# A fused window-attention and gated-MLP kernel: new hand-written orders for all engines, with own and preceding scores merged from the fifth block on

## The chip, the cores and the metric

The kernel runs on one core of a Trainium2 chip. Five engines work side by side, each through its own list of instructions in a fixed order: TensorE (PE in the profile; its weight loads are PEld), VectorE (DVE), ScalarE (ACT), GpSimd (POOL, "Pool" here) and SyncE (SP), which does nothing here but issue transfers. Transfers are carried out by 16 DMA engines. An engine's next instruction waits until its semaphores are reached; whatever stands behind it in that engine's list waits with it. Time is device microseconds for one execution, start to end.

## What is computed

Attention over a sliding window of 128 keys and 4 "sink" keys, for 4 batches of 8 heads, 768 tokens, 64 values per head; its output, 3072 tokens of 512 values, goes through a two-layer network with the gate h * sigmoid(1.702 h) and 2048 hidden values.

```python
scores = scale * np.matmul(q, k.transpose(0, 1, 3, 2))
keep = is_sink | in_window            # first 4 keys, or 0 <= query - key < 128
scores = np.where(keep, scores, -1e9)
a = np.exp(scores - scores.max(-1, keepdims=True))
a = a / (a.sum(-1, keepdims=True) + 1e-9)
x = (a @ v), heads side by side: 3072 x 512
h = x @ w_in                          # 512 x 2048
out = (h / (1 + np.exp(-1.702 * h))) @ w_out
```

## The kernel before

**Blocks, positions and groups.** The 3072 tokens are 24 blocks of 128, six for each batch. They are worked on in the order ORD (L26): blocks 0, 6, 12, 18 (the first of each batch, which have no preceding block and no separate sink), then 1, 2, 3, 4, 5, 7, 8 and so on. A place in that order is called a position here, from 0: position 4 is block 1, 5 is block 2, 6 is block 3, 7 is block 4, 8 is block 5, 9 is block 7, 10 is block 8, 11 is block 9, 12 is block 10, 13 is block 11. Two positions make a group: group 2 is positions 4 and 5, group 4 is positions 8 and 9.

**One block's way.** Pool loads q, k and v, cast to 16 bits (L298, L289; block 0's q and k come through SyncE and ScalarE and are cast on the chip). q and k are transposed: on TensorE with an eviction by VectorE or ScalarE for positions 0 to 7 (L391), by a DMA transposition issued by SyncE for two positions at once from 8 on (L412). TensorE makes the scores against the block's own keys (`own`), against the preceding block's (`prv`) and against the four sink keys (L490). Only one of own and prv counts for each pair of query and offset, so VectorE picks between the two with a mask (`pack`, L514), takes the maximum (L526, L542), subtracts it (L583, L598), and ScalarE takes the exponential (L616; the first four positions take half of it from the scores directly, L569, and have their mask added on TensorE, L438). The result `a` is transposed into `at`: on TensorE for positions 0 to 3 (L679), by a DMA transposition issued by SyncE from position 4 on (L717). Pool then splits it into the weights for the preceding block and for the own block by two selects (L628, L622), 1.1 us each. TensorE multiplies with v (the "attention" of a position, in two halves `av0` and `av1`: L738 for the sinks, which uses `vsb`, then L744 and L748), VectorE normalises (L759, L760), and the result goes to `xT` by a TensorE transposition and an eviction (L773; positions 0 to 7) or a DMA transposition (L786; from group 4 on).

`vsb` is made once for each batch by VectorE or Pool (L346) from the first four rows of v, which SyncE loads (`vsa`, L341); every position from 4 on needs that of its batch.

**The network.** For each group TensorE does the first layer in eight parts `h0` to `h7` of 8 matmuls (group 0: 16 short ones each, four parts for each of its two blocks), ScalarE the gate on each (L838), and TensorE the second layer in two rows of four parts, `o0.0` to `o1.3` (L859), of which part n needs the gates of parts 2n and 2n + 1 and the quarter n of w_out. VectorE or ScalarE evicts, SyncE stores (L877). The exponential and the gate each need their own table on ScalarE; a change of table takes 1.28 us (ACT_TABLE_LOAD).

**What sets the order.** Every operation is added to a plan with a number (in the order in which the source adds them), a cost and a list of what it depends on. The plan's costs, margins (`late`, `post`), keys and `deps` were used to search for an order; in this file the result is written out, and nothing reads them any more. `ORDER` (L40) lists the operations by number with the engine's letter (P, A for ScalarE, V for VectorE, G for Pool, S for SyncE), and the last lines of the function emit them in that order; the tile framework then puts the semaphores, from the order of emission and from what each instruction reads and writes. Where two operations touch the same PSUM bank, the later one in the list waits for the earlier. `FILL` puts that many extra matmuls on zeros in front of an operation on TensorE, and `HOME` moves PSUM tiles from their usual ring of banks to another (`mm`, 3 banks, for transposes and the network; `own`, 2; `pv`, 2, for prv and av).

**Scores in one operation.** From position CFG["merge"] on, own and preceding scores are one operation (L466 to L478): its 16 matmuls alternate between the two, and it takes its four PSUM banks at once. Below, they are two operations.

**The order around the change, decoded.** TensorE, from the second-layer work of groups 0 and 1 on (S: scores, av: both halves where not numbered, Tx: transposition to xT): o1.3(g1) o1.2(g0) | av5 av4 | o1.3(g0) Tx5 av0-6 Tx4 S8 av1-6 | h of group 2, with sinks of 8 in between | Tx6 av7 o0.0 S9 o0.1 Tx7 ... Pool: loads q18, k18, the identity, q12, the mask bias0, k12, v18, v0, v6, q1, k1, v12, three parts of w_in, k2, q2, the fourth, q3, k3, k4, q4, four parts of w_out, q5, q7, k5, vsb of batch 1, v3, k7, v2, v1, then selects of positions 5, 4 and 6, six loads, select of 7, six loads, select of 8, two loads, select of 9. (k6 and q6 come first.) ScalarE: all 16 gates of groups 0 and 1, then the exponentials of positions 5, 4, 6, 7. SyncE: transpositions of `at` for 5 and 4, the load of vsa for batch 0, the transposition for 6, q and k of positions 8 and 9, and so on.

Of the kernel before, what the change touches and what calls it, by code (L numbers as in the profile page):

```python
# [29 lines left out]
PE, ACT, DVE, POOL, SP = "PE", "ACT", "DVE", "POOL", "SP"  # L30
CFG = dict(
    tq=(0, 1, 2, 3, 4, 5, 6, 7), ta=(0, 1, 2, 3), tx=tuple(range(8)), nb={0: 1, 1: 1, 2: 1, 3: 1}, wide=(1, 3),
    split=(0,), gbatch={}, tanh=(), after0=25.0, vsb=15.0, slack=dict(v=1.0, s=1.0, x=1.0, e=0.0, p=0.0), merge=8, pemask=(0, 1, 2, 3), f32=(0,), sel2=(), fill=(1.5, 45.0, 0.15, 0.11), chain=99, gap=3, steady=8, after=8.0,
# [7 lines left out]
9V 2V 18V 16V 4V 13V 19V 17V 12V 23G 0S 1S 7S 22G 28G 29G 3G 15V 11V 26G 21A 20V 108P 109V 110P 5G 10V 113P 27G 132P  # L41
133A 111V 112V 114P 130P 116V 32G 24G 25G 36G 37G 131A 118A 115V 31G 117V 174P 135P 136P 137V 119A 122P 175A 176P
139V 120P 138V 121V 152P 177A 154P 179P 33G 180P 123V 153A 141A 142P 155A 140A 35G 157P 182V 181V 184A 30G 41G 40G
124P 158P 183V 185A 159V 161V 126P 143A 34G 163A 144P 160V 127V 186P 162A 145V 187V 125V 164P 188P 146P 198P 189V
147V 165A 128P 129A 148P 149V 190P 191V 168P 196P 197A 192P 166P 150P 199A 582P 193V 194P 167V 169V 170P 151A 202P
590P 171V 583A 46G 47G 50G 49G 172P 173V 586P 594P 195A 178A 39G 38G 620P 591A 587A 595A 201P 200P 222P 612P 6S 203V
220P 221A 621A 614P 613A 615A 204V 223V 205V 206V 14V 207V 134V 208V 210V 608P 588P 592P 609A 589A 593A 209V 42G 43G
52G 55G 53G 584P 246P 618P 247V 585A 8S 101S 105G 48G 56G 45G 244P 270P 245V 225P 271V 224P 228V 610P 226P 619A 268P
580P 44G 616P 269A 581A 230V 227V 229V 231V 233V 622P 617A 232V 234V 248P 249P 251V 252V 253V 596P 623A 611A 235A
630P 250P 254V 255V 258V 256V 236S 631P 624P 257V 211A 259A 274P 597P 212S 625P 272P 273P 632P 275V 100S 260S 276V  # L50
277V 278V 279V 281V 626P 598P 280V 237G 627P 628V 292S 602P 599P 603P 213G 633P 282V 283A 604P 634A 635S 284S 600A
601S 104V 240P 261G 238P 241V 216P 214P 239V 605P 215V 217V 242P 62G 51G 606A 262P 243A 218P 607S 293P 219V 264P 58G
67G 65G 61G 285G 646P 294P 296V 295V 263V 297V 647A 265V 298V 299V 636P 640P 650P 300V 301V 302V 651A 648P 649A 644P
637A 645A 638P 642P 641A 639A 59G 266P 286P 288P 643A 267V 287V 289V 303A 652P 310P 312V 313V 653P 290P 57G 86G 54G
64G 68G 291A 304S 658P 314V 315V 311P 659P 328S 316V 674P 319V 318V 660P 317V 320A 676P 661P 664P 678P 677A 675A
321S 305G 71G 364S 662A 654P 73G 329P 665A 679A 102S 331V 322G 333V 655P 668P 669A 332V 308P 334V 672P 95G 309V 330P
325P 673A 74G 335V 306P 326V 666P 70G 323P 336V 337V 667A 670P 324V 307V 63G 79G 686P 671A 338V 327S 346P 339A 687P
680P 688P 347P 348V 349V 351V 350V 656A 340S 352V 353V 106G 681P 629S 355V 354V 689P 696P 356A 690A 382P 341G 60G
697A 657S 357S 384V 385V 682P 383P 692P 683P 386V 80G 693A 400S 103S 387V 388V 389V 390V 698P 694P 699A 78G 365P
695A 684A 702P 367V 358G 369V 704P 368V 370V 391V 705A 703A 700P 344P 366P 69G 76G 66G 77G 345V 371V 701A 361P 708P  # L60
392A 362V 359P 373V 714P 360V 342P 706P 393S 343V 372V 709P 715P 374V 363S 375A 418P 685S 707A 716P 376S 420V 394G
422V 710P 421V 436S 156A 717P 423V 419P 711P 718V 424V 425V 427V 722P 663S 712A 426V 83G 720P 726P 401P 723A 721A
728P 403V 724P 402P 729A 405V 377G 107V 75G 404V 725A 406V 730P 731A 72G 82G 88G 81G 397P 398V 407V 395P 732P 733A
727A 380P 734P 742P 396V 90G 408V 410V 428A 381V 378P 379V 736P 399S 743P 409V 411A 737P 735A 412S 454P 744P 456V
429S 738P 457V 713S 455P 739P 745P 458V 459V 89G 85G 472S 460V 413G 746A 462V 461V 748P 463V 437P 749A 754P 439V
752P 755A 430G 92G 414P 753A 740A 415V 440V 442V 441V 438P 758P 762P 750P 416P 443V 84G 96G 91G 94G 445V 433P 759A
756P 417V 444V 434V 751A 763A 770P 757A 464A 431P 764P 760P 432V 446V 435S 741S 490P 447A 765P 761A 448S 491P 766P
493V 492V 494V 495V 771P 465S 496V 499V 767P 768A 508S 691S 778P 769S 449G 497V 772P 779A 498V 788P 473P 789A 466G
784P 785A 475V 476V 474P 773P 477V 478V 479V 87G 98G 99G 452P 780P 781A 482V 774A 776P 467P 790P 97G 468V 481V 782P
791A 453V 777A 480V 469P 450P 786P 451V 470V 798P 787A 471S 775S 783A 526P 500A 792P 529V 528V 799P 527P 531V 530V  # L70
793P 483A 501S 532V 800P 533V 535V 794P 484S 534V 536A 806P 795P 807A 537S 502G 509P 801P 544S 511V 485G 802V 513V
796A 512V 510P 808P 505P 809A 810P 514V 747S 818P 811A 93G 506V 486P 538G 804P 487V 503P 805A 812P 816P 504V 813A
819A 515V 516V 517V 488P 814P 826P 489V 507S 815A 817A 562P 518V 519A 565V 564V 820P 827P 563P 520S 567V 566V 568V
828P 821P 571V 569V 829P 834P 570V 572A 545P 822P 830V 521G 835A 803S 831S 842P 573S 547V 548V 823P 843A 550V 549V
524P 824A 832P 546P 551V 554V 553V 846P 574G 525V 838P 847A 833A 552V 539P 540V 541P 840P 542V 844P 839A 841A 577P
836P 837A 848P 522P 523V 555A 854P 543S 849P 855P 845A 556S 850P 719S 797S 856P 575P 851P 557G 868P 576V 852A 857P
853S 869A 862P 858A 860P 870P 560P 861A 561V 863A 578V 866P 864P 871A 558P 865A 872P 559V 867A 882P 873A 876P 825S
579S 883P 877P 874P 878P 875A 884P 879P 892P 880V 885P 881S 893A 894P 886V 888P 887S 895A 859S 890P 889A 898P 891A
896P 899A 902P 910P 897A 900P 903A 911P 901A 904P 912P 905P 916P 906P 917P 907P 913P 908V 918P 914A 919P 909S 915S
920A 921S  # L80
# [3 lines left out]
    map(int, x.split(":"))  # L84
    for x in """
108:16 110:2 174:7 154:3 144:11 164:4 128:2
""".split()
)

HOME = dict(x.split(":") for x in "0:own 2:pv 6:own 8:own 10:pv 12:own 16:own 17:own 19:pv 20:pv 22:mm 25:own 26:own 27:mm 28:mm 29:own 32:pv 35:pv 38:own 39:pv 41:pv 43:own 45:own 46:mm 49:mm 50:mm 52:mm 53:mm 54:own 56:pv 57:mm 59:own 60:mm 61:mm 62:mm 64:own 66:mm 67:own 69:own 70:mm 168:own 170:pv 173:pv 174:own 177:pv 178:pv 179:pv 181:own 183:own 185:pv 187:pv 188:pv 191:pv 192:own 195:pv 197:pv 203:pv 204:own".split())  # L90

class Buf:


# [54 lines left out]
def kernel(  # L151
# [30 lines left out]
    plan = Plan(RING)  # L182
# [32 lines left out]
    raw, o_raw = {}, {}  # L215
# [709 lines left out]
```

## Time and profile before

| | us |
|---|---|
| median of 3 runs | 230.03 (230.0 to 230.13) |
| the profiled execution | 229.54 |
| its span in the profile | 227.8 |
| TensorE busy | 216.8 (95%) |
| VectorE, ScalarE, Pool busy | 136.0, 127.3, 114.3 |
| TensorE's granted clock | 1.00 in every stretch |
| the first matmul of the first layer | 20.79 |
| the end of the last matmul | 224.57 |

The profile shows one execution. Its page gives the engines' busy times, and the span in 40 slices of 5.7 us with the busy share of each in tenths. The timeline lists instructions with start and duration, merges equal neighbours (x8: eight of them), and says in brackets how long the engine had been idle before and what ended that: `[1.75 <-DVE vsb L346]` is 1.75 us idle until VectorE's instruction of line 346, which writes vsb, was done. `at<-a` reads: at is written from a. A row of SPq, the queue of SyncE, is the time that SyncE spent on issuing a transfer, not the transfer's own; "to landing" is from issue to the end of the transfer.

### The profile page before, as it was taken

How to read it: one execution, taken by the hardware profiler on the slowest of the kernel's cores; microseconds unless marked ns; L12 is line 12 of the kernel's file. 1: busy time of each engine (PE TensorE's matmuls, PEld its weight loads, DVE VectorE, ACT ScalarE, POOL GpSimd, SP SyncE). 2: the span in 40 equal slices, each digit the busy share in tenths (PEclk: the TensorE clock that was granted, in tenths of full speed). 3: DMA queues.
4: the chain of work that ended last, by engine and by line, in shares of the span. 5: the costliest groups of instructions: out<-in, count | busy, mean ns of one | idle time of the engine just before them, and what ended most of it. 6: DMA issues, size and time to landing. Idle time of an engine off the chain costs nothing.

```text
span 227.8 us, 5439 instructions
## 1 busy us (share of the span) xinstructions
PE 216.8 (95%) x2237; PEld 153.0 (67%) x2237; DVE 136.0 (60%) x334; ACT 127.3 (56%) x196; POOL 114.3 (50%) x126
## 2 busy tenths in 40 slices
PE   6789999996999999899999999999999999999994
PEld 4568998444785684585685695685695695775862
DVE  5799389674858188576875876577587751131101
ACT  2689675711584836757539359347646738441621
POOL 7995575118994594692794490570570430300000
PEclk9999999999999999999999999999999999999999
DMA  9999999999999999999999999998982703620302
GB/s 134 148 159 204 181 187 206 168 142 228 175 108 143 217 116 141 202 166 112 241 148 149 223 97 171 195 147 125 183 138 54 192 0 71 214 42 7 138 0 92
DMA packets 131992, 32.82 MB, mean 144 GB/s; under 512 B 124640, under 2 KB 129024, under 8 KB 131968
## 3 DMA queue, kind: packets, MB, share of 16 engines
q0 software_dynamic: 77024, 13.37, 77.6%
q1 hardware_dynamic: 53904, 18.85, 41.2%
q10 hardware_dynamic: 1040, 0.26, 0.5%
q8 instruction: 17, 0.28, 0.5%
q14 instruction: 7, 0.06, 0.1%
HBM read 27.36 MB, written 6.29 MB: 148 GB/s over the span
## 4 chain that ended last, share of the span: by engine, by line
PE 62%; DMA 16%; POOL 11%; issue 6%; DVE 1%; ACT 1%; POOLq 0%; SPq 0%
PE hT L808 28%; PE o L859 25%; DMA w_out<-in_moe_w_out_dram 6%; DMA w_in<-in_moe_w_in_dram 5%; POOL qkn L298 3%; DMA xT<-xn 3%; DMA at<-a 3%; POOL at L622 3%; POOL atp L628 2%; POOL v L289 2%; PE own L471 2%; PE av L744 2%; PE av L748 2%; PE av L738 1%; PE prv L471 1%
## 5 line engine op out<-in xcount | busy, mean ns | idle before, releaser
L808 PE MATMUL hT<-xT,w_in 128*128 128x256 f16 (+1 forms) x832 | 93.3, 264 | 0.9 <-DMA xT<-xn 0.9
L859 PE MATMUL o<-w_out,gT 128*128 128x512 f16 (+1 forms) x400 | 91.0, 371 | 0.0
L808 PEld LDWEIGHTS <-w_in 128*128 128x128 f16 x832 | 73.6, 98 | 13.0 <-DMA xT<-xn 1.4
L838 ACT ACTIVATE gT<-hT 128x512 f16<-128x512 f32 x96 | 54.7, 599 | 49.4 <-PE hT L808 49.0
L859 PEld LDWEIGHTS <-gT 128*128 128x128 f16 x400 | 36.8, 98 | 33.8 <-ACT gT L838 0.2
L628 POOL TENSOR_SCALAR_AFFINE_SELECT atp<-at 128x1024 f16<-128x1024 f16 x20 | 22.0, 1098 | 70.2 <-DMA at<-a 59.4
L514 DVE COPY_PREDICATED own<-later,prv 128x512 f32<-128x512 uint16 x40 | 26.5, 692 | 30.8 <-PE prv L471 25.9
L616 ACT ACTIVATE a<-e 128x1056 f16<-128x1056 f32 (+1 forms) x24 | 24.1, 1014 | 16.9 <-DVE e L598 7.1
L526 DVE TENSOR_REDUCE mx<-own 128x4 f32<-128x512 f32 x48 | 31.7, 685 | 1.6 <-PE own L446 1.1
L583 DVE TENSOR_TENSOR e<-own,mx 128x512 f32<-128x512 f32 x44 | 29.2, 684 | 0.8
L289 POOL DMA_DIRECT2D v<-in_v_dram x24 | 21.5, 899 | 3.3 <-DMA w_out<-in_moe_w_out_dram 3.3
L622 POOL TENSOR_SCALAR_AFFINE_SELECT at<-at 128x1024 f16<-128x1024 f16 x20 | 22.2, 1110 | 1.4
L298 POOL DMA_DIRECT2D qkn<-in_q_dram x23 | 20.7, 904 | 2.1 <-DMA w_in<-in_moe_w_in_dram 1.6
L298 POOL DMA_DIRECT2D qkn<-in_k_dram x23 | 20.8, 906 | 1.7 <-POOLq L906 0.8
L760 DVE TENSOR_TENSOR xn<-av,rcp 128x256 f16<-128x256 f32 x48 | 20.4, 425 | 1.7
L271 ACT COPY osb<-o 128x512 f32<-128x512 f32 (+1 forms) x18 | 10.0, 560 | 19.4 <-PE o L859 18.9
L759 DVE RECIPROCAL rcp<-av 128x4 f32<-128x4 f32 x48 | 8.5, 177 | 19.2 <-PE av L748 19.1
L744 PE MATMUL av<-v,at 128*128 128x65 f16 x192 | 16.9, 194 | 1.0 <-POOL at L622 0.7
L744 PEld LDWEIGHTS <-at 128*128 128x128 f16 x192 | 14.1, 98 | 5.2 <-POOL atp L628 2.0
L267 DVE COPY osb<-o 128x512 f32<-128x512 f32 x7 | 4.8, 690 | 19.8 <-PE o L859 19.5
L748 PE MATMUL av<-v,atp 128*128 128x65 f16 x160 | 15.0, 194 | 0.0
L838 ACT ACT_TABLE_LOAD x10 | 12.8, 1283 | 0.2
(62 smaller groups left out, 167.0 us busy)
## 6 DMA issues: line engine op xcount, KB each, us to landing
out_dram<-osb SPq DMA_DIRECT2D x23, 256.0 KB, 2.5
v<-in_v_dram POOLq DMA_DIRECT2D x24, 128.0 KB, 4.8
qkn<-in_k_dram POOLq DMA_DIRECT2D x23, 128.0 KB, 5.3
qkn<-in_q_dram POOLq DMA_DIRECT2D x23, 128.0 KB, 5.2
w_in<-in_moe_w_in_dram POOLq DMA_DIRECT2D x4, 512.0 KB, 10.1
w_out<-in_moe_w_out_dram POOLq DMA_DIRECT2D x4, 512.0 KB, 12.6
at<-a SPq DMA_TRANSPOSE x20, 4.7
rawq<-in_q_dram SPq DMA_DIRECT2D x1, 256.0 KB, 3.9
```

The lines of the kernel that those rows point to most:

```text
L289: return sw(key, 0.88, lambda: nc.gpsimd.dma_start(v65[:, b, :, 0:D], src), 1.0, deps=[z_1] + deps, after=after)
L298: key, 0.88, lambda: nc.gpsimd.dma_start(buf()[:, i, w], src), 0.9,
L514: nc.vector.copy_predicated(out=own[l](), mask=later.unsqueeze(1).to_broadcast((P, 4, P)), data=prv[l]())
L526: lambda l=l, own=own, small=small, r=r: nc.vector.tensor_reduce(out=small[:, l], in_=own[l](), axis=AX.X, op=ALU.max, negate=r == 0),
L583: nc.vector.tensor_tensor(out=e32()[:, 512 * l : 512 * l + 512].rearrange("p (j s) -> p j s", j=4), in0=own[l](), in1=small[:, l].unsqueez ...
L616: nc.scalar.activation(out=a16()[:, lo:hi], in_=e32()[:, lo:hi], func=AF.Exp, scale=factor)
L622: nc.gpsimd.affine_select(out=dst()[:, lo : lo + n], in_=at()[:, lo : lo + n], pattern=[[0, n], [1, P]], compare_op=ALU.is_ge, fill=0.0, b ...
L628: nc.gpsimd.affine_select(out=dst()[:, lo : lo + n], in_=at()[:, lo : lo + n], pattern=[[0, n], [-1, P]], compare_op=ALU.is_gt, fill=0.0, ...
L744: nc.tensor.matmul(av()[:, j], ato()[:, c], v65[:, b, h], start=(r == 0), stop=(r == 0))
L808: nc.tensor.matmul(ht()[:, n], w_in16[:, c, bass.ts(f, P)], xt[g]()[:, tok, c], start=(c == 0), stop=(c == 3))
L838: lambda fs=fs, cols=cols, gt=gt, ht=ht: nc.scalar.activation(out=gt()[:, fs[0] : fs[-1] + 1, cols], in_=ht(), func=AF.Gelu_apprx_sigmoid),
L859: nc.tensor.matmul(po(), gt()[:, F, bass.ts(t, P)], w_out16[:, F, cols], start=(F == 0), stop=(F == NF - 1))
```

## The change

The written-out order, the fillers and the homes of the PSUM tiles are replaced by others, `merge` goes from 8 to 4, and some costs that only the search read are changed:

```diff
-    ... merge=8, ...
+    merge=4,
...
-108:16 110:2 174:7 154:3 144:11 164:4 128:2
+108:18 130:2 132:1 174:3 154:2 157:8 126:6 188:2 164:1 166:3
...
-            o_raw[w, b] = hw(-3000, 0.4, ..., 0.7, late=1.15 if w == "q" else 0.5)
+            o_raw[w, b] = hw(-3000, 0.4, ..., 0.7, late=1.15 if w == "q" else 0.3)
...
     o_ident = plan.add(
-        POOL, -2003, 0.35,
+        POOL, -2003, 0.3,
...
             key, 0.88, lambda: nc.gpsimd.dma_start(buf()[:, i, w], src), 0.9,
-            take=[buf], after=after, deps=deps,
+            take=[buf], after=after, deps=deps + [o_bias0],
...
-            o_ks[bb] = plan.add({DVE: 0.5, ACT: 0.5}, K0 - 39.5, 0, sink_keys, ...)
+            o_ks[bb] = plan.add({DVE: 0.75, ACT: 0.5}, K0 - 39.5, 0, sink_keys, ...)
```

The `late=`, cost and `deps` values are the search's. ORDER has four operations fewer (the preceding scores of positions 4 to 7 are now in the own scores' operation). Decoded, the new order differs in these places:

| Engine | before | after |
|---|---|---|
| Pool, start | k6 q6 q18 k18 identity q12 bias0 k12 v18 v0 v6 q1 k1 v12 | bias0 q6 k6 q18 k18 identity k12 q12 v0 v18 q1 k1 v6 v12 |
| Pool, weights | w_in parts 1, 3, 0, k2 q2, part 2, q3 k3 k4 q4, w_out 1, 0, 2, 3, q5 q7 k5, vsb, v3 k7 v2 v1 | w_in parts 3, 1, 2, q2 k2, part 0, q3 k5 k3 k4 q4, w_out 0, q7, w_out 1, vsb, w_out 2, 3, k7 q5 v1 v2 |
| Pool, selects | 5, 4, 6, six loads, 7, six loads, 8, two loads, 9 | 5, 4, nine loads (v4, v3 second and third), 6, four loads, 7, one load, 8, five loads, 9 |
| TensorE, start | fillers 16, 2, 7, 3, 11, 4, 2; first layer begins with part 1 of group 0 | fillers 18, 2, 1, 3, 2, 8, 6, 2, 1, 3; first layer begins with part 7 of group 0 |
| TensorE, q and k of positions 6 and 7 | before the last first-layer part of group 1 | q of 6 before it, the other three behind it |
| TensorE, attention | av5, av4, Tx5, av0-6, Tx4, S8, av1-6, h of group 2, Tx6, av7, o0.0, S9 | av5, o1.2(g0), av4, Tx5, o1.3(g0), Tx4, S8, five h of group 2, S9, three h, o0.0 o1.0, av0-6, o1.1 o0.1 o1.2, av1-6, av1-7, o0.2, av0-7, o1.3, Tx6 Tx7 |
| TensorE, before the first layer of group 4 | S11 o1.1 o0.0 o1.2 o0.1 o1.3 | S11 o1.1 o0.2 o1.2 o0.3 o1.3 S13 |
| ScalarE | exponentials of 5, 4, 6, 7 | exponentials of 4, 5, 6, 7 |
| SyncE | `at` of 5, 4, load of vsa, `at` of 6 | `at` of 5, load of vsa, `at` of 4, 6 |
| VectorE | vsb of batch 0 after all of position 7's subtractions | vsb of batch 0 ahead of position 7's subtractions |

More of the change, by code (lines that the diff above doesn't have):

```diff
@@ L31 @@
 CFG = dict(
-    tq=(0, 1, 2, 3, 4, 5, 6, 7), ta=(0, 1, 2, 3), tx=tuple(range(8)), nb={0: 1, 1: 1, 2: 1, 3: 1}, wide=(1, 3),
-    split=(0,), gbatch={}, tanh=(), after0=25.0, vsb=15.0, slack=dict(v=1.0, s=1.0, x=1.0, e=0.0, p=0.0), merge=8, pemask=(0, 1, 2, 3), f32=(0,), sel2=(), fill=(1.5, 45.0, 0.15, 0.11), chain=99, gap=3, steady=8, after=8.0,
+    tq=(0, 1, 2, 3, 4, 5, 6, 7),
+    ta=(0, 1, 2, 3),
+    tx=(0, 1, 2, 3, 4, 5, 6, 7),
+    nb={0: 1, 1: 1, 2: 1, 3: 1},
+    wide=(1, 3),
+    split=(0,),
+    gbatch={},
+    tanh=(),
+    after0=25.0,
+    vsb=15.0,
+    slack={'v': 1.0, 's': 1.0, 'x': 1.0, 'e': 0.0, 'p': 0.0},
+    merge=4,
+    pemask=(0, 1, 2, 3),
+    f32=(0,),
+    sel2=(),
+    fill=(1.5, 45.0, 0.15, 0.11),
+    chain=99,
+    gap=3,
+    steady=8,
+    after=8.0,
     loads="q0 k0 q6 k6 v0 v6 q12 k12 q18 k18 i0 v12 v18 i1 i2 i3 q1 k1 o0 o1 q2 k2 o2 o3 v1 v2".split(),
@@ L46 @@
[L46 to L55, printed above, removed]
@@ L76 @@
[L76 to L80, printed above, removed]
+9V 4V 0S 17V 2V 15V 5G 13V 1S 22G 11V 19V 101S 18V 12V 7S 23G 6S 8S 28G 29G 20A 21A 3G 27G 108P 110P 109A 10V 113P
@@ L231 @@
     o_bias0 = plan.add(
-        POOL, -2002, 0.35,
+        POOL, -2002, 0.3,
         lambda: nc.gpsimd.affine_select(
@@ L427, in sink_keys @@
                     copy(e, ksb[rows, bb, :, 4 * hl : 4 * hl + 4], qk_of(b)[rows, 4:8, 0:4])
-            o_ks[bb] = plan.add({DVE: 0.5, ACT: 0.5}, K0 - 39.5, 0, sink_keys, deps=o_qkt[b] + [z_k], give=[home[b]])
+            o_ks[bb] = plan.add({DVE: 0.75, ACT: 0.5}, K0 - 39.5, 0, sink_keys, deps=o_qkt[b] + [z_k], give=[home[b]])
         own = [ps("mm" if n in CFG["wide"] else "own", (P, 4, P), FP32, f"own{b}_{l}") for l in range(2)]
```

67 lines of the change are left out of this document (40 added, 27 removed).

## The prediction

> **What bounds the kernel now.** Positions are counted as in the text above: position 4 is block 1, position 5 block 2. I read the page's first two parts, then the idle gaps of TensorE in order of time, then the engine or queue that ended each gap.
>
> ```profile
> PE 216.8 (95%) x2237; PEld 153.0 (67%) x2237; DVE 136.0 (60%) x334; ACT 127.3 (56%) x196; POOL 114.3 (50%) x126
> ...
> DMA  9999999999999999999999999998982703620302
> ```
>
> TensorE is busy 216.8 of 227.8 us; the other 11.0 us is all that a new order can win. The DMA engines are full for the first 28 of 40 slices, so early transfers come when the queue lets them. TensorE's timeline, the rows that begin after a gap (start, length, and in brackets the idle time and what ended it):
>
> ```profile
> 20.79 1.06 PE L808 MATMUL hT<-xT,w_in 128*128 128x128 f16 x16
> ...
> 54.94 0.27 PE L738 MATMUL av<-vsb,at 128*128 128x260 f16 x1 [1.75 <-DVE vsb L346]
> ...
> 58.11 0.20 PE L744 MATMUL av<-v,at 128*128 128x65 f16 x1 [0.24 <-POOL at L622]
> ...
> 82.65 0.20 PE L744 MATMUL av<-v,at 128*128 128x65 f16 x1 [0.50 <-POOL at L622]
> ...
> 92.40 1.05 PE L808 MATMUL hT<-xT,w_in 128*128 128x256 f16 x8 [0.94 <-DMA xT<-xn]
> ```
>
> Three stages: the start until the first gated layer at 20.79 (about 4.3 us idle and 45 filler matmuls); four gaps between 53 and 93, together 3.43 us; after 93 none until the last 3.2 us, which evict and store. The gap at 53.2 ends with a small table, vsb of the first batch, whose input was asked for late. From the timeline of all engines, SyncE's queue (SPq) and VectorE:
>
> ```profile
> 43.80 4.27 SPq L717 DMA_TRANSPOSE at<-a  x1
> ...
> 48.12 0.71 SPq L341 DMA_DIRECT2D vsa<-in_v_dram  x1
> ...
> 53.40 1.49 DVE L346 TENSOR_TENSOR vsb<-vsa,ownm 32x520 f16<-32x520 f32 x1 [3.25 <-DMA vsa<-in_v_dram]
> ```
>
> Right behind that gap stands another limit. Pool's timeline, the last loads and the selects of positions 5 and 4:
>
> ```profile
> 38.24 0.88 POOL L289 DMA_DIRECT2D v<-in_v_dram  x1 [1.68 <-DMA w_out<-in_moe_w_out_dram]
> 40.76 0.88 POOL L289 DMA_DIRECT2D v<-in_v_dram  x1 [1.64 <-DMA w_out<-in_moe_w_out_dram]
> 50.41 1.09 POOL L628 TENSOR_SCALAR_AFFINE_SELECT atp<-at 128x1024 f16<-128x1024 f16 x1 [8.78 <-DMA at<-a]
> 51.57 1.09 POOL L622 TENSOR_SCALAR_AFFINE_SELECT at<-at 128x1024 f16<-128x1024 f16 x1
> 53.25 1.09 POOL L628 TENSOR_SCALAR_AFFINE_SELECT atp<-at 128x1024 f16<-128x1024 f16 x1 [0.58 <-DMA at<-a]
> 54.41 1.43 POOL L622 TENSOR_SCALAR_AFFINE_SELECT at<-at 128x1024 f16<-128x1024 f16 x1
> ```
>
> The transposed weights of position 5 land at 50.35, of position 4 at 53.2 (9.4 us after SyncE took them up at 43.80; the least in this trace is 3.3), and the selects of 4 end at 55.84. TensorE's attention of position 4 starts its selected part at 55.90: I call this moment X. Everything before X fills time; everything after X is paid.
>
> **The change, part by part.** The new costs and margins in the calls, and the added dependency of loads on bias0, only fed the planner; the order is written out, so they emit nothing: 0. The merge drops no matmul. One merged operation at 58.68 lasts until 59.23, 0.55 us; the separate pair at 26.09 lasts until 26.64, 0.55 us: 0. It asks for four PSUM banks at once; in the walks below the banks are free first, the closest by about 0.3 us at position 9. 46 fillers against 45 stand before the first layer, where the chain below decides: 0. The end is the same: both store the last two half tiles after the last matmul: 0.
>
> *Start.* Pool puts bias0 (0.31) ahead of all loads and ident behind four of them: loads +0.25, ident ready at 5.6 instead of 5.36. The second transpose of block 0 no longer waits for an eviction (it ran at 6.31 behind one; now 6.1). ScalarE then has the eviction of q0 and a sink copy more, VectorE two evictions more before the first exponentials. Following both engines with the rows' steps (eviction 0.36 VectorE, 0.49 ScalarE; maximum or subtraction 0.6; normalise 0.55; four-part exponential 1.05; plain one 0.55) VectorE is the one without pauses from 14.4 on, its eviction of the transposed block of position 1 ends at 20.6, and the first layer starts at 20.75 instead of 20.79: 0, with +-0.5. The weights must be there: Pool's waits show w_in parts landing at about 20.0, 22.5, 25.0 and 29.3; the new order uses its first three at 20.8, 22.8 and 27.5 and the last at 30.1, close but in time.
>
> *To X.* Three transposes of q and k (0.22 each) move behind the last first-layer work of groups 0 and 1, and one short product less is open at the start: the last gelu ends 0.8 us earlier. But the new order runs two exponentials (1.03 each) before the first transposition is issued, where the old ran one, and the sum gives an issue at about 42.0 against 42.16. The load of vsa (0.71) now stands between the two transpositions: the second is taken up at about 44.2 against 43.80, 0.4 later. In exchange vsb is made at about 48 while Pool waits, so the 1.75 gap's cause is gone; what is late next is the select of position 5, then 4. One load, v of block 3, moves from before the transpositions to behind them. With transpositions and loads together the queue moves about 150 GB/s, so 128 KB less is worth at most 0.87 us for the later landing. Against that stand the 0.4 of the later take-up and more of w_out in the queue at 42: Pool's waits show a part of w_in or w_out landing every 2.5 us, the third of w_out at 40.47, so the last at about 42.8; k of block 5 and q of block 7 (0.85 each at 150 GB/s) now go ahead, so 44.5. I take the second landing 0.25 earlier (ends -0.87 and +1.7). And the second select at 54.41 took 1.43 against 1.09 elsewhere, while VectorE made vsb in 1.49 (another vsb took 0.68); now they are apart: -0.34. X moves by -0.6; range -1.2 to +1.7.
>
> The Trainium skill, GPSIMD Engine Reference, section 1, says Pool shares its memory ports with VectorE and collides with VectorE operations of two SBUF inputs, as vsb is; the 1.43 against 1.09 agrees, and by the rule the saving of 0.34 stays. The Trainium skill, DMA: Bandwidth & Descriptors, "Queues, rings and completion order", says each DMA engine alternates between queues, one packet at a time; by it the larger packets of w_out cost the transposition more than block loads would, which speaks against the change and is the second rival's mechanism.
>
> *From X to 93.* At X the set of finished TensorE work is the same in both orders. From X to the first layer of group 4 the old order takes 36.50 us, of them 1.68 idle (0.24, 0.50, 0.94). Its pieces by the rows (first layer 0.873, second 0.866, attention half 0.355, scores 0.5) sum to 33.8, so real time is 1.03 of such a sum. New order: Pool issues nine loads (0.883), select 6 (2.22), four loads, select 7: 7.95 + 2.22 + 3.53 + 2.22 = X + 15.9. TensorE reaches attention of position 7 after 15.24 x 1.03 = 15.7: it waits 0.3 (0 to 0.7). Position 8's transposition is taken up at about X + 13.2 and lands 6.3 later, as the one at 69.96 did, so its select ends at X + 21.8, needed at X + 26; position 9's behind five loads at X + 28.4, needed at X + 29.9. The last attention of position 9 ends at X + 30.9, its normalise at X + 31.6, the transposition to xT lands 3.0 to 6.3 later (the trace's least and most; the most was this very one), X + 34.6 to 37.9; TensorE has other work until 36.02 x 1.03 + 0.3 = 37.4: it waits 0 to 0.5, I take 0.3. So 0.6 idle instead of 1.68: -1.1 (range -1.7 to -0.5). Loads moved behind selects must land too: v of block 3, issued at X + 2.7, is needed at X + 12.6; 5 us is the usual landing, 13.1 the longest.
>
> *After 93.* The old order never waits there. The new one leaves 18 to 30 us of TensorE work between scores and attention (13.8 at position 11, 14.3 before, and the old one lived with 13.1 at position 9 at the price of 0.5), and 6.3 to 7.5 between the last attention of a group and its first layer (5.6 to 7.8 before): 0, with up to +0.5 at position 11.
>
> Sum: 0 - 0.6 - 1.1 = -1.7. The profiled execution took 229.54 us, span 227.8 and 1.74 around it: 227.84 for its like. The median of the runs shown is 230.03, 0.49 above: 228.3.
>
> **Rivals.** *It evens out.* The first transposition's issue slips by an exponential and X by +0.5 to +1.5, which eats the later gain. For it: the exponentials are swapped, and any slip at the start goes straight to the issue. Time 228.3 + 0.6 + 1.1 = 230.0.
> *Slower: the transpositions lose to w_out.* If the first one moves little until w_out's last part is in (44.5 - 42.8 = 1.7 us later), X moves by +1.7; select 6 and all behind it too, and with the gap at X + 36.6 at its worst the later gain is 0.5: 230.03 + 1.7 - 0.5 = 231.2. Against it: the block loads behind are fewer. It decides from X + 1.6 on.
> *Pool's loads hold the selects.* Between 20 and 41 Pool stopped six times for 0.7 to 1.75 us until an earlier load had landed; each time about eight loads were out. Nine loads now stand ahead of select 6. Two such stops delay select 7 by 3.3 us: 228.3 + 3.3 = 231.6. Against it: between 58 and 71 Pool issued twelve loads without a stop.
> *More.* All waits go but the one at X: -1.2 and -1.7: 227.1.
>
> **How the numbers follow.** About 0.2%, 0.46 us, is what a measurement can tell from no change. Forecast 0.54 (228.3, its own range 227.3 to 229.5), more 0.08, evens out 0.13, transpositions lose 0.16, Pool's loads 0.09. Faster 0.62, same 0.13, slower 0.25. From 226.9 to 231.3 the range leaves out Pool's loads, a part of the slower case and the rim of the best one.
>
> **What would show it.** Right: no gap ended by vsb; first layer at 20.3 to 21.3; transpositions of 5 and 4 taken up near 42.0 and 44.2; X near 55.3, ended by a select of position 4; a gap under 0.7 at attention of position 7; under 0.5 before group 4; none after 93. Wrong: transposition 4 landing after 54; Pool idle among the loads behind select 4; a first-layer matmul waiting for w_in or w_out; gaps on TensorE after 93.

## The result, and the profile after

The changed kernel takes 227.42 us (median of four runs, 226.91 to 228.61), the kernel before 230.03 (230.0 to 230.13) on the same chip. The ratio is 0.9901, with a 95% interval of 0.9875 to 0.9926: one per cent faster, where the prediction said 228.3. The profiled execution happens to be the slowest of the four, 228.61 us with a span of 226.9, so against the profiled execution of before (229.54, span 227.8) only 0.93 us are seen. Executions of the changed kernel differ by 1.7 us here, those of before by 0.13 (in the experiments below, by up to 3). So this pair of profiles holds 0.9 of the 2.6 us between the medians; what the faster executions did differently stands in no trace.

The first and second part of the page of the changed kernel, busy times and the DMA engines' slices:

```profile
PE 218.1 (96%) x2238; PEld 153.7 (68%) x2238; DVE 138.7 (61%) x332; ACT 127.0 (56%) x197; POOL 115.3 (51%) x127
...
DMA  9999999999999999899997999998998175202202
```

TensorE is idle for 8.8 us instead of 11.0, but it counts as busy 1.3 us longer. Where these 1.3 us sit is not shown. TensorE's timeline, the first row of the first layer, and then every row behind it that begins after a gap of over 0.15 us. Line numbers are 17 higher than before (L622 is L639, L808 is L825).

```profile
20.82 1.39 PE L825 MATMUL hT<-xT,w_in 128*128 128x128 f16 x22
...
54.56 0.20 PE L761 MATMUL av<-v,at 128*128 128x65 f16 x1 [0.38 <-POOL at L639]
...
62.42 0.21 PE L488 MATMUL own<-qkT 64*128 64x128 f16 x1 [0.38 <-DVE e L600]
...
71.15 0.27 PE L755 MATMUL av<-vsb,at 128*128 128x260 f16 x1 [0.63 <-DVE e L600]
...
132.00 1.25 PE L825 MATMUL hT<-xT,w_in 128*128 128x256 f16 x10 [0.34 <-DVE osb L284]
```

The gaps of before are gone: none ends with vsb, none stands before the first layer of group 4 (it begins at 92.73 without a wait), and none at the attention of positions 6 and 9 ends with a select. X is at 54.56, 1.34 earlier than in the kernel before, where the row is:

```profile
55.90 0.20 PE L744 MATMUL av<-v,at 128*128 128x65 f16 x1
```

Three gaps are new (the one at 71.15 is ahead of the second half of position 6), and all of them end with a subtraction or an eviction of VectorE's, an engine that ended none of the gaps shown of before but that of vsb. Pool's timeline around the first selects, positions 5 and 4, and the loads behind them:

```profile
49.62 1.09 POOL L645 TENSOR_SCALAR_AFFINE_SELECT atp<-at 128x1024 f16<-128x1024 f16 x1 [12.59 <-DMA at<-a]
50.78 1.51 POOL L639 TENSOR_SCALAR_AFFINE_SELECT at<-at 128x1024 f16<-128x1024 f16 x1
52.25 1.09 POOL L645 TENSOR_SCALAR_AFFINE_SELECT atp<-at 128x1024 f16<-128x1024 f16 x1
53.41 1.09 POOL L639 TENSOR_SCALAR_AFFINE_SELECT at<-at 128x1024 f16<-128x1024 f16 x1
54.45 0.89 POOL L315 DMA_DIRECT2D qkn<-in_k_dram  x1
55.33 1.76 POOL L306 DMA_DIRECT2D v<-in_v_dram  x2
57.06 1.79 POOL L315 DMA_DIRECT2D qkn<-in_q_dram  x2
58.80 0.92 POOL L315 DMA_DIRECT2D qkn<-in_k_dram  x1
59.67 0.93 POOL L306 DMA_DIRECT2D v<-in_v_dram  x1
60.53 1.81 POOL L315 DMA_DIRECT2D qkn<-in_k_dram  x2
62.27 1.18 POOL L645 TENSOR_SCALAR_AFFINE_SELECT atp<-at 128x1024 f16<-128x1024 f16 x1
```

Before, Pool waited twice, for the transposed weights of position 5 and 0.58 us more for those of position 4. Now the four selects run one behind the other from the first landing on, and the second landing no longer counts. The nine loads behind them are issued without a stop. SyncE's queue shows when the transpositions of positions 5 and 4 were taken up, with the load of vsa between them (x2 in the last row: position 4's and the next):

```profile
42.04 1.51 SPq L734 DMA_TRANSPOSE at<-a  x1
43.61 0.77 SPq L358 DMA_DIRECT2D vsa<-in_v_dram  x1
44.49 5.13 SPq L734 DMA_TRANSPOSE at<-a  x2
```

One select still takes 1.51 us instead of 1.09. What it meets is on VectorE:

```profile
49.54 0.19 DVE L559 TENSOR_REDUCE ms<-misc 128x8 f32<-128x32 f32 x1 [1.03 <-PE misc L507]
49.77 0.96 DVE L562 TENSOR_TENSOR mx<-mx,ms 128x8 f32<-128x8 f32 x1
50.66 0.68 DVE L363 TENSOR_TENSOR vsb<-vsa,ownm 32x520 f16<-32x520 f32 x1
```

vsb is made at 50.66, not at 48: in VectorE's list it stands behind the maxima of position 7, which waited until 49.54 for TensorE's scores against the sinks. And a combine of 8 columns (L562, the greater of the row maxima and the sinks' maxima), which takes 0.17 us elsewhere, takes 0.96. It ends at 50.73; Pool's select that was running when it began ends at 50.72.

**Where the time went.** At X the same TensorE work is finished in both orders, so a run divides there: when X comes, and how long the rest takes up to the start of the last matmul (224.30 before, 223.46 after). Most later readings rest on this split. Waits are the gaps of over 0.15 us behind X, from TensorE's timeline; "combine" is the time that VectorE's combine took beyond 0.17 us in the executions behind X in which it took over 0.2.

| kernel (one profiled execution each) | select of 5 begins | X | X to the last matmul | waits | combine |
|---|---|---|---|---|---|
| before | 50.41 | 55.90 | 168.40 | 1.68 | 0.11 |
| after | 49.62 | 54.56 | 168.90 | 1.35 | 2.67 |

So in this pair of executions the whole gain lies ahead of X. Behind X, 0.5 us were lost, where the prediction had a gain of 1.1. One pair of traces is not enough for more: the profiled execution of after is the slowest of its four, and that of before is 0.5 us faster than its median.

### The profile page after: what moved, and what is told of

It reads as the page before. It is cut to its first block, busy times and chain, and to the rows that moved or that the text cites. A ratio compares the mean times of both kernels' runs of the same rounds, so it can differ in the third digit from the quotient of the medians.

```text
span 226.9 us, 5434 instructions
## 1 busy us (share of the span) xinstructions
PE 218.1 (96%) x2238; PEld 153.7 (68%) x2238; DVE 138.7 (61%) x332; ACT 127.0 (56%) x197; POOL 115.3 (51%) x127
## 4 chain that ended last, share of the span: by engine, by line
PE 85%; DVE 7%; POOL 3%; ACT 2%; issue 1%; POOLq 0%; DVEq 0%
PE hT L825 35%; PE o L876 35%; PE own L488 3%; PE av L761 2%; PE av L765 2%; PE prv L488 2%; PE av L755 2%; DVE mx L562 2%; DVE mx L543 1%; POOL qkn L315 1%; PE tq L408 1%; DVE e L600 1%; POOL at L639 1%; ACT a L586 1%; PE tx L790 1%
## 5 line engine op out<-in xcount | busy, mean ns | idle before, releaser
L825 PE MATMUL hT<-xT,w_in 128*128 128x256 f16 (+1 forms) x832 | 91.9, 264 | 0.3 <-DVE osb L284 0.3
L825 PEld LDWEIGHTS <-w_in 128*128 128x128 f16 x832 | 74.0, 98 | 11.9 <-issue 0.7
L639 POOL TENSOR_SCALAR_AFFINE_SELECT at<-at 128x1024 f16<-128x1024 f16 x20 | 22.3, 1113 | 1.4
L288 ACT COPY osb<-o 128x512 f32<-128x512 f32 (+1 forms) x17 | 9.2, 561 | 19.3 <-PE o L876 13.2
L284 DVE COPY osb<-o 128x512 f32<-128x512 f32 x8 | 5.5, 688 | 18.5 <-PE o L876 18.1
L488 PEld LDWEIGHTS <-qkT 64*128 64x128 f16 x320 | 9.4, 94 | 7.0 <-issue 5.7
```

The costliest lines, as they stand in the source:

```text
L639: nc.gpsimd.affine_select(out=dst()[:, lo : lo + n], in_=at()[:, lo : lo + n], pattern=[[0, n], [1, P]], compare_op=ALU.is_ge, fill=0.0, b ...
L825: nc.tensor.matmul(ht()[:, n], w_in16[:, c, bass.ts(f, P)], xt[g]()[:, tok, c], start=(c == 0), stop=(c == 3))
```

## Experiments

Each was run beside the kernel before on the same chip (median of before 229.98 in the first four, 230.55 in the next four, 230.54 in the last four; single runs 229.1 to 232.5, a wider spread than in the result). The ratio given with a run is the recorded one, with its 95% interval; it can differ from the quotient of the two medians by up to 0.0025. Diffs of the written-out order are given in the names of the table of the change, not in its numbers. "After" is the changed kernel.

### The changed kernel again

No edit.

> The changed kernel once more, unaltered. Its first four executions lay between 226.91 and 228.61, a spread of 0.75% where the kernel before spreads by 0.06%. Theory one (a collision that is hit or missed by a few hundredths of a microsecond: VectorE's small combine of two SBUF tiles, 0.17 us, took 0.96, 1.06, 1.10, 0.34 and 0.86 us where it began inside one of Pool's selects or loads): the spread comes back, 226.8 to 228.7, and in this profile the gaps on TensorE near 62, 71 and 132 stand only where that combine is long. Theory two (the spread is in the transfers before X): the gaps at 62, 71 and 132 are the same whatever the time, and X, 54.56 in the first profile, moves with it.

Measured: 228.38 us (227.28 to 229.14, eight runs), ratio 0.9911 (0.9877 to 0.9945). Its profile: select of position 5 at 50.39, X at 55.24, rest 168.01, with waits of 0.70 and 1.91 us of lengthened combines. Both parts move from one execution to the next: X by 0.7, with the last load ahead of it landing at 50.15 instead of 48.97, and the rest by 0.9, with the combines. So both theories hold in part: the combine near 60 is short this time and the gap at 62 is gone, the one near 130 is long again and its gap is there, and X moves by itself. What comes out of one trace of this kernel is good to about a microsecond, and the runs below are read by the split and not by their totals alone.

### Small maxima in PSUM: the changed kernel and the kernel before

```diff
-    smalls = const.tile([P, 2, 4], FP32, name=f"ms{b}")
+    smalls = misc[:, 32:40].rearrange("p (l j) -> p l j", l=2)
```

The sinks' maxima go to eight unused columns of the PSUM tile of the sinks' scores, so the combine reads one operand from SBUF and one from PSUM. Nothing else is changed.

> The changed kernel with one edit: the maximum over the four sink scores is written to a corner of PSUM instead of SBUF, so that VectorE's combine reads one tile from SBUF and one from PSUM. Theory one (the combine of two SBUF tiles waits for the end of Pool's select and so holds up the subtractions that free TensorE's banks): the combine takes 0.17 to 0.2 everywhere, the gaps at 62.42 (0.38), 71.15 (0.63) and 132.00 (0.34) are gone, the profiled time falls by 1.0 to 1.4 against a profile that has them, median 226.0 to 226.8, spread under 0.4%. Rival (the combine is long for another reason, such as its own wait for the sinks' scores): it stays at 0.3 to 1.1 in those places and the time is that of the changed kernel, 227.4 +- 0.5.

> The kernel before, with nothing but the small maxima of the sinks in PSUM. Theory: the meeting of VectorE's combine with Pool's work is a cost that the new order brought; in the profiled execution of before it happened once, for 0.28 us, and ended no wait of TensorE. So nothing moves: ratio 0.998 to 1.002. Rival: the collisions cost the old order as much as the new one, and the ratio falls to about 0.993, as it did between the changed kernel and its like with the small maxima in PSUM.

Measured: the changed kernel 226.88 us (226.24 to 226.99), ratio 0.9841 (0.9805 to 0.9878); the kernel before 230.26 (229.85 to 231.28), ratio 0.9996 (0.9974 to 1.0018). In neither does any combine take over 0.2 us. The changed kernel's median is just above the 226.0 to 226.8 expected. The only gap on TensorE behind the start that is left in the changed order:

```profile
54.73 0.20 PE L761 MATMUL av<-v,at 128*128 128x65 f16 x1 [0.38 <-POOL at L639]
```

X is where it was without the edit (54.73; select of position 5 at 49.87), the rest takes 167.05 instead of 168.0 to 168.9 (and 167.06 in a second kernel with the same edit, below). So the three new gaps were made by the lengthened combine: it holds up the subtractions and evictions behind it, which free the PSUM banks that TensorE's next scores, attention or first layer write. Without it the new order's rest is 1.35 us shorter than that of before, where 1.1 was predicted. In the order of before the same edit is worth nothing (its rest, 169.57, is not shorter): there the combine met a select once, for 0.11 us beyond its time. The rival, that the collisions cost the old order as much, fell. The rows of the changed kernel that show such a meeting, VectorE's and then Pool's timeline:

```profile
69.27 1.10 DVE L562 TENSOR_TENSOR mx<-mx,ms 128x8 f32<-128x8 f32 x1
70.40 1.29 DVE L600 TENSOR_TENSOR e<-own,mx 128x512 f32<-128x512 f32 x2
...
130.16 0.86 DVE L562 TENSOR_TENSOR mx<-mx,ms 128x8 f32<-128x8 f32 x1
```

```profile
69.26 1.09 POOL L639 TENSOR_SCALAR_AFFINE_SELECT at<-at 128x1024 f16<-128x1024 f16 x1
...
129.88 1.11 POOL L645 TENSOR_SCALAR_AFFINE_SELECT atp<-at 128x1024 f16<-128x1024 f16 x1
```

The first select ends at 70.35 and the combine at 70.37; the second at 130.99 and 131.01. Of the 23 combines that took over 0.2 us in five profiles of the changed order (after, its second execution, and the runs with two operations, with w_out ahead and with v of block 3 ahead), all but two end 15 to 31 ns after a select that was running when they began. The other two, at 59.99 here and at 60.63 in a run below, stood beside two load issues of Pool's and no select; what held them is open. With the small maxima in PSUM the combine in that place, at 60.17, took 0.16 us. The Trainium skill, SBUF — State Buffer, section "SBUF: two separate sides", says that VectorE and GpSimd share a pair of SBUF ports as an exclusive lock: of a VectorE operation with two SBUF inputs and a GpSimd operation that reads SBUF, the one that starts first has the pair for its whole length, and the other is blocked until it ends. The 15 to 31 ns between the two ends agree, and so does the cure: with one input in PSUM no combine took over 0.2 us.

### v of block 3 (and of block 4) ahead of the selects

```diff
 # Pool's order, the changed kernel
-    ... k7 q5 v1 v2, selects 5 and 4, k8 v4 v3 ...
+    ... k7 q5 v3 v1 v2, selects 5 and 4, k8 v4 ...        (one load)
+    ... k7 q5 v3 v4 v1 v2, selects 5 and 4, k8 ...        (two loads)
```

> The changed kernel with one load moved back: v of block 3 ahead of v of blocks 1 and 2, before the selects, as in the order before. The last load ahead of X landed at 48.97 to 50.15 in the changed kernel's profiles, 53.0 in the old one's. If v3 is what keeps the queue busy behind the transpositions, the last load lands 1.3 to 2 later, position 4's transposition (landed at 50.57 and 51.27) after 52, and X moves by 0.3 to 0.9: 228.0 to 229.0 beside 227.4 to 228.4. Rival (it is the order of w_out and the block loads, not v3): position 4 lands before its select's turn, X within 0.2, the time of the changed kernel.

> The changed kernel with two loads, v of block 3 and v of block 4, ahead of the first selects instead of behind them. Putting v of block 3 alone there moved X by 1.1 to 1.8 us. Theory: each block load ahead of the transpositions costs them the time of its own 256 KB read and 128 KB written in a full queue, so the second costs as much again: X at 57 to 58, 2 to 3.5 us later than in the changed kernel, time about 231 (ratio 1.00 to 1.01). Rival: the one load mattered because it was the last of those that the transposition still met; a second adds at most the 0.87 us that the prediction had for it, X at about 56.5 to 57, time about 230 (ratio 0.998 to 1.001).

Measured: one load 229.51 us (229.12 to 230.62), ratio 0.9975 (0.9953 to 0.9997); two loads 229.77 (229.19 to 231.23), ratio 0.9972 (0.9947 to 0.9997). The loads of Pool's queue behind the last part of w_out, and when each landed, from the trace's DMA issues:

| kernel | last of w_out | the loads behind it | select of 5 begins | X |
|---|---|---|---|---|
| after (4 loads) | 44.35 | 45.23 46.06 47.64 48.97 | 49.62 | 54.56 |
| v3 ahead (5) | 44.71 | 45.75 46.66 48.67 49.80 52.29 | 51.48 | 56.33 |
| v3 and v4 ahead (6) | 44.78 | 45.73 46.74 48.63 50.41 51.72 53.87 | 52.11 | 56.96 |
| before (7) | 43.03 | 43.87 44.72 45.68 46.77 48.42 50.50 53.00 | 50.41 | 55.90 |

The first two of these loads (before: the first three) land 0.83 to 1.04 us behind the one ahead of them. The later ones, with the transpositions moving too (their first packets move at 45.3 to 46.6 in these four traces), take 1.1 to 2.5. What the DMA engines moved from 44 to 54 us, in slices of 0.25 us, in the changed kernel and, in the second fence, with v3 ahead:

```profile
GB/s 149 155 157 153 154 161 164 191 203 135 84 59 36 20 55 209 181 174 101 214 260 144 290 280 290 288 290 277 177 217 202 219 211 224 216 212 200 243 415 401
```

```profile
GB/s 148 151 153 156 154 153 154 154 150 152 175 200 176 114 78 38 11 10 48 163 185 182 183 120 119 117 138 133 135 106 106 110 174 283 244 207 290 273 269 221
```

In both, the transfers almost stop for 1.25 us (20 to 84 GB/s from 46.5 on, 10 to 78 from 47.5 on with v3 ahead); what stops them is not shown. Then they part. In the changed kernel the last load lands at 48.97, and from 49.5 to 51.0 the transpositions move 277 to 290 GB/s. With v3 ahead its load and the transpositions share 106 to 138 GB/s from 49.75 to 52.0, and 283 come only when it is in. The mean of 150 GB/s that priced v3 hides all of this. So v3 behind the selects is worth 1.1 to 1.8 us of X (56.33 against 55.24 and 54.56), more than the 0.3 to 0.9 expected and not the 0.87 at most that 128 KB at 150 GB/s gave. The second load adds 0.63 to X and hardly any time (0.26 us, on another chip), as its rival said. With v3 ahead, X in the new order is 0.4 us later than before, less than it moves between executions: without the place of this one load, nothing is gained ahead of X.

### w_out ahead, as before

```diff
 # Pool's order, the changed kernel
-    k5 k3 k4 q4, w_out 0, q7, w_out 1, vsb, w_out 2, 3, k7 q5 ...
+    k3 k4 q4, w_out 0, 1, vsb, w_out 2, 3, q7 k5 k7 q5 ...
```

> The changed kernel with all four parts of w_out ahead of the loads of k of block 5 and q of block 7, as in the kernel before; the number of loads ahead of the first selects is the same. Theory: what counts for X is how many bytes are ahead of the transpositions, not which: X within 0.4 us of the changed kernel, time 227.0 to 228.2, ratio 0.988 to 0.992. Rival (the second of the prediction, large packets delay a transposition more than block loads do): with w_out in the queue earlier the transpositions meet less of it, the first lands 0.5 to 1.7 us earlier and X with it, time 226 to 227.

Measured: 228.02 us (227.87 to 229.28), ratio 0.989 (0.9857 to 0.9922); select of position 5 at 50.34, X at 55.19, rest 168.74. w_out's last part landed at 42.77 instead of 44.35, and nothing came of it: X is within 0.1 us of the changed kernel's second execution and 0.6 behind the first. With the same loads ahead of the selects, it made no difference that can be measured whether w_out is among the earlier ones. The rule that engines alternate between queues by the packet, on which the prediction's second rival stood (the Trainium skill, DMA: Bandwidth & Descriptors, "Queues, rings and completion order"), isn't contradicted, but w_out's larger packets cost nothing here that can be measured.

### vsb earlier: before, and the changed kernel with the small maxima in PSUM

```diff
 # SyncE's order, the kernel before
-    at of 5, at of 4, load of vsa, at of 6
+    at of 5, load of vsa, at of 4, at of 6
```

```diff
 # VectorE's order, the changed kernel with the small maxima in PSUM
-    ... maxima of 7, small maximum of 7, vsb, subtractions of 7 ...
+    ... maxima of 7, vsb, small maximum of 7, subtractions of 7 ...
```

> The kernel before with one load moved: vsa of batch 0 between the transpositions of positions 5 and 4, as in the changed kernel. My reading of the old profile: the gap ended by vsb goes, but the selects of position 4 stand behind it; X goes from 55.9 to 55.5 at best (the select no longer meets VectorE's vsb, 0.34) and to 56.2 at worst (the second transposition is taken up later): 229.6 to 230.3. Rival (vsb's lateness is the cost, as the old profile's longest gap says): 1.5 to 1.75 faster, 228.3.

> The changed kernel with the small maxima of the sinks in PSUM, and with VectorE's vsb of the first batch moved ahead of the last small maximum of position 7. Theory: vsb then runs at about 48, while Pool still waits for the transposed weights of position 5; both of the first selects take 1.09 us (1.43 and 1.51 in the runs in which vsb meets them), X comes 0.34 us earlier than with the small maxima alone, and all of it is paid: about 226.5 us, ratio about 0.983. No subtraction of VectorE's stands behind a select, so TensorE has no gap of over 0.2 us but the one at X. Rival: X is held by the landing of the transposition of position 4 and not by the chain of selects; the select of 4 waits for it and the time stays at that of the small maxima alone, 226.9.

Measured, the first: 229.96 us (229.27 to 230.46), ratio 0.9973 (0.9956 to 0.9991). The gap of vsb, 1.75 us before, is gone; in its place TensorE waits for the selects of position 4 (line numbers are one lower here than before):

```profile
55.48 0.20 PE L743 MATMUL av<-v,at 128*128 128x65 f16 x1 [1.32 <-POOL at L621]
```

X moves by 0.4: the selects begin at 50.63 and no longer wait for the landing of position 4, but one of them still takes 1.43. So the gap that the profile of before showed largest was worth a quarter of its length at X. This is as the prediction read it: right behind it stood another limit.

Measured, the second: 226.74 us (226.34 to 227.25), ratio 0.9836 (0.9805 to 0.9867), no more than with the small maxima alone. VectorE's timeline shows why:

```profile
49.93 1.39 DVE L363 TENSOR_TENSOR vsb<-vsa,ownm 32x520 f16<-32x520 f32 x1 [1.42 <-DMA vsa<-in_v_dram]
```

VectorE now reaches vsb at 48.5 and waits for vsa, which SyncE took up at 44.34: vsb begins 5.6 us later, when the transposition of position 5 has landed too (its first select begins at 49.68). With vsa behind that transposition vsb was not ready ahead of the select, and the second select is lengthened to 1.43 us again. X is at 54.53, 0.2 earlier than with the small maxima alone, and a gap of 0.35 that ends with a subtraction of VectorE's stands at 53.10, where none was expected. The time is the rival's, but not for its reason: the transposition of position 4 landed at 50.64, and its select begins at 52.23 without a wait. Loading vsa ahead of both transpositions was not tried.

### The merge alone, and undone

```diff
 # before: one operation for own and preceding scores from position 4 on
-    merge=8
+    merge=4
 # after: two again for positions 4 to 7
-    merge=4
+    merge=8
```

> The kernel before with one part of the change: own and preceding scores of positions 4 to 7 in one operation, put where the later of the two stood; all else as before. My prediction: 0, so 230.0 +- 0.3. Rival (the merge carries the gain, because the picks start sooner): 0.5 us or more faster. A third way (four banks at once block TensorE between 26 and 45): slower only if the loss reaches X, since everything ahead of X has 1.75 us of idle to spend: 230.0 to 230.5.

> The changed kernel with the merge undone: own scores and preceding scores of positions 4 to 7 as two operations, one right behind the other, in the place of the merged one; order and banks otherwise as changed. My prediction: the merge is worth 0, so the changed kernel's time, 227.4 +- 0.6. Rival (the merge carries the gain): 228.5 to 230.

Measured: before with the merge 230.28 us (229.64 to 231.14), ratio 1.0001 (0.9977 to 1.0024), X at 56.09, rest 168.72; after without it 227.56 (227.19 to 229.06), ratio 0.9886 (0.9841 to 0.993), X at 54.53, rest 168.30. The merge is worth nothing either way.

### Half of each order

```diff
 # first: everything as before up to the attention of position 5, then the new order
 # second: everything new up to X (v of block 3 loaded ahead, since the old rest needs it), then the old order
```

> The order before up to the attention of position 5 (own and preceding scores of positions 4 to 7 apart, v of block 3 loaded early), and the changed order for all that is left: nine loads ahead of select 6, attention of position 6 late, and so on. So only the second term of my sum, behind X. By the sum -1.1 (ends -1.7 to -0.5): 228.9 on a kernel before of 230.0, with X where it was, 55.9. By the first profile of the changed kernel, where the stretch from X to the end gave 0.8 less: 229.2. Rival (all of the gain is ahead of X): 230.0 +- 0.3.

> The other half: the changed order up to the attention of position 5, then the order before for the rest; v of block 3 is loaded ahead of v of block 1, since the old rest needs it soon. So only the first term, to X, without the later place of v3. By my sum -0.6; by the profile of the changed kernel X came 1.34 earlier, so 228.7 if v3 is worth nothing, 229.5 if v3 is worth the 0.87 that I gave it. Rival (the gap at vsb was the cost): 228.3, the whole 1.75. Rival (none of the gain is here): 230.0 +- 0.3.

Measured, the first: 230.83 us (230.0 to 231.75), ratio 1.0009 (0.9986 to 1.0033); X at 57.41, rest 168.90, of it 1.26 of waits, with 1.99 us of lengthened combines. The second: 230.66 (229.59 to 231.6), ratio 1.0005 (0.9985 to 1.0026); X at 56.90, rest 168.64. Neither half by itself is faster than the kernel before. As traces, neither is a clean measure of its parts. The first has a wait of 1.05 us for a load of k at 27.82, which before doesn't have, so its X is no measure of the old beginning. In the second, TensorE's granted clock was 0.50 from 56.9 to 60.3, right behind X, so its rest is no measure of the old rest (columns: start and end, length, busy time of each engine, granted clock, DMA share, GB/s):

```profile
57.00:58.00 1.00, 1.00 (x18) 0.94 (x18) 0.00 (x0) 0.00 (x0) 0.93 (x2) 0.50 0.99 289
```

The times say more. The second hybrid and the run with v3 ahead have the same beginning, up to the attention of position 5, and ran on the same chip; one goes on with the old rest, the other with the new one. The medians are 230.66 and 229.51, the ratios 1.0005 and 0.9975. So the new rest is worth 0.7 to 1.15 us, although its combines are lengthened by 1.7 us in that trace. The new beginning with v3 ahead is worth nothing (230.66 beside 230.55 of before). What is left is the place of v3: the ratio is 0.9975 with it ahead and 0.9901 and 0.9911 without, 1.5 to 1.7 us. Each ratio is uncertain by 0.2 to 0.35%, 0.5 to 0.8 us, so the two medians of one chip are the firmest of these. Put together, the place of v3, the new rest and nothing from what remains of the beginning make 2.2 to 2.9 us, where 2.0 to 2.6 were measured for the whole change. The traces agree only roughly: the new rest takes 167.9 to 168.9 in them, the old one 168.4 to 169.6 where the clock is whole.

## Why the prediction was right, and where it was wrong

*Start, 0.* Right: the first layer began at 20.82 (20.75 predicted; 20.75 to 21.26 in the other traces of the new beginning), and no first-layer matmul waited for w_in.

*To X, -0.6.* Measured -1.34 and -0.66 in two executions, and X at 54.53 to 54.73 in three runs with edits that leave its loads alone. The sign holds; two of its terms fail.
The second transposition's landing was put 0.25 us earlier, and came 2.6 earlier (50.57 against 53.19; 51.27 in the second execution). The term that was mis-sized is v of block 3, "worth at most 0.87" by the mean rate of the queue. Beside transpositions a load takes up to 2.5 us, transpositions move 106 to 138 GB/s beside it and up to 290 without it, and one load less moved X by 1.1 to 1.8. Against it the later take-up (44.49 and 45.37 instead of 43.80, where 44.2 was predicted) took some back: with v3 ahead again the new order's X is 0.4 later than before, in one trace. Since the gain of the landing was larger than thought, the chain changed its head: X is now the landing of position 5 and four selects behind it, and the landing of position 4 is hidden.
The saving of 0.34 from a select that no longer meets vsb did not come: vsb was put at about 48, and was made at 50.66, behind a combine that waited for TensorE's scores against the sinks; it was made at 49.93 where VectorE was ready for it at 48.5, because vsa itself came late. The prediction's own row had a warning: vsa was taken up at 48.12 before and vsb began at 53.40, 5.3 us later; 43.61 and 5.3 is 48.9, beside a landing of the weights at 49.6 no safe distance.

*From X to 93, -1.1.* The mechanism was right, and partly hidden by something else. The waits named are gone, the one before group 4 among them (xT landed at 91.02, the first layer began at 92.73), and none stands at the attention of position 7, where 0.3 each had been left. Behind the same beginning the new rest was 0.7 to 1.15 us faster than the old one. That this meets the 1.1 is in part luck, since with the small maxima in PSUM the rest is 1.35 shorter than in the trace of before. The step that failed is "the banks are free first, the closest by about 0.3 us at position 9": the walk had no term for a lengthened combine of VectorE's. The new order runs it beside Pool's selects and loads four or five times behind X (1.7 to 3.1 us in all), and that holds the banks at 62.42, 71.15 and 132.00. It gave back 1.0 to 1.85 us (168.01 and 168.90 against 167.05). The prediction knew of such a meeting, for vsb, and priced it at one place alone.

*After 93, 0.* Wrong by the 0.34 at 132.00, the same cause. *Merge, fillers, end, 0.* The merge was measured as 0; nothing in the traces speaks against the others.

*The rivals.* "It evens out" needed the first transposition to slip; it was taken up at 42.04 (42.0 predicted), and at 42.29 in the second execution. "The transpositions lose to w_out" fell in the run with w_out ahead. "Pool's loads hold the selects" fell with the nine loads issued without a stop. The medians, 227.4 and in the second comparison 228.4, stand on both sides of the forecast of 228.3, and that it fits so well is in part luck: two errors of opposite sign met. v3 was worth more than predicted, and the collisions, not predicted, took back part of what the rest gained.

The version with the small maxima in PSUM is faster than both kernels: 226.88 against 228.38 for the changed kernel on the same chip, and 0.9841 of before.

Open: why X differs by 0.7 us between executions of the same program (the last load ahead of it landed at 48.97 and 50.15); what held the two combines beside load issues; what stops the transfers for 1.25 us; and vsa ahead of the transpositions.

## What to carry to other kernels

When an order is changed, walk through which operations of VectorE's with two SBUF inputs will now run beside Pool's work: an instruction of 0.17 us can cost a whole select, and it is paid by whoever needs what stands behind it. A transfer that is taken out of a full queue can be worth more than its bytes at the mean rate, when the transfer on the path would have met it; price it by the spacing of the landings in that stretch. And where a large gap ends with one input, look for the next limit right behind it: here 1.75 us of gap were worth 0.4 at X. When two halves of a change are run apart, compare each with a run that shares its other half, and look at the granted clock first.

## What was not expected of the hardware

- A combine of two SBUF tiles, 128x8, takes 0.17 us alone and up to 1.10 beside a select of Pool's; it ends 15 to 32 ns after the select. With one operand in PSUM it never took over 0.2.
- Block loads land 0.83 to 1.04 us apart until the transpositions move and 1.1 to 2.5 beside them. A load and DMA transpositions share 106 to 138 GB/s; the transpositions alone moved 277 to 290. Every trace of the changed order looked at has a stretch of 1 us or so there in which hardly anything moves.
- A small load of 32 partitions on SyncE's queue (vsa) took 4.5 to 8.5 us from its take-up to the start of what waits for it, over eleven traces, while that stretch was full.
